# First score group of a causal attention: 112 and 224 key columns instead of 256

## The chip, the cores and the metric

The kernel runs on one core of one Trainium2 chip. The metric is the device time of one execution in microseconds (us); the time of a kernel is the median over its runs. Shapes are written as partitions x elements, and `128x448` for a matmul means 128 contraction rows and 448 moving columns.

## The reference, cut to what matters

A causal attention (2 batches, 12 heads, 448 positions, head size 64) is followed by two MLP-mixer-like blocks, the second with a two-dimensional Fourier transform and a layer normalisation. The change touches the attention alone:

```python
scores = scale * np.matmul(q, k.transpose(0, 1, 3, 2))          # 448 x 448 for each head
mask = np.triu(np.ones((seq, seq), dtype=bool), k=1)
scores = np.where(mask, -1000000000.0, scores)
scores = scores - np.max(scores, axis=-1, keepdims=True)
attn = np.exp(scores)
attn = attn / (np.sum(attn, axis=-1, keepdims=True) + 1e-09)
return np.matmul(attn, v)
```

Query block `i` of 112 positions needs only the first `112 * (i + 1)` keys; all later ones are masked.

## The kernel before, in words

The 24 heads of both batches are worked on as 12 pairs. Of a pair, one head's 64 rows of q and k lie in partitions 0 to 63 and the other's in 64 to 127, so that two matmuls, one for each head (`e` in the code), lie in two halves of TensorE's array. The 448 queries are cut into four blocks of 112.

For precision q and k are split into a high and a low part (`qh`, `ql`, `kh`, `kl`, type fp32r, a rounded fp32), and each score is the sum of three matmuls: high times high, high times low, low times high.

`scores(n, g)` makes the scores of pair `n` in three groups: `g` = 0 holds query blocks 0 and 1, `g` = 1 block 2, `g` = 2 block 3. The results of a group lie in one PSUM bank for each head. In group 0 block 1 stands in columns 0 to 255 and block 0 in columns 256 to 511. After the products, matmuls of a bf16 identity with a bf16 mask (line 234) add -1e9 above the diagonal. VectorE takes the negated maximum of each row (line 238), and ScalarE makes the exponential with that maximum as its bias and sums the row (line 247). Both read only the `112 * (i + 1)` columns that the block needs; line 214 sets the width of the matmuls on its own:

```python
for i, c0 in zip(blocks, cols):
    w = max(256, TS * (i + 1))
```

With `TS` = 112 that gives 256, 256, 336 and 448 columns for the four blocks. Line 221 is the matmul of these products.

The order of TensorE's instructions is written out by hand in a loop over `n`: scores group 0 of pair `n`, then the product with the values (`pv`, line 275, plain fp32) of pair `n` - 2, scores group 1 of pair `n`, and then transposes of the probabilities (line 260) of pair `n` - 1 around scores group 2, with parts of the first mixer block (lines 321, 333, 355) and the transposes of the outputs (line 296) put between. VectorE and ScalarE carry the softmax, copies out of PSUM (lines 265 and 267), and the conversion of float64 weights to two fp32r parts (lines 75 to 93). The feed-forward layers behind the attention (lines 134 to 136 and 497 to 499) are long rows of matmuls of 448 columns. Line 709, in a later stage, multiplies by a single column to get variances.

Of the kernel before, what the change touches and what calls it, by code (L numbers as in the profile page):

```python
# [21 lines left out]
TS = 112  # L22
# [18 lines left out]
def fused_kernel(ctx: ExitStack, tc: tile.TileContext, qk, v, w1, w2, wa, wb, wc, wd, fa, fa0, fb, out):  # L41
# [100 lines left out]
    with ExitStack() as actx:  # L142
        ps = actx.enter_context(tc.tile_pool(name="aps", bufs=2, space=bass.MemoryType.PSUM))

        def ybank():
            return ps.tile([128, 512], F32, tag="y", name="b_y")
# [56 lines left out]
        def scores(n, g):  # L203
            c = pairs[n]
            if g == 0:
                c.ssum = ap.tile([TS, NI, 2, 1], F32, tag="ssum", name="ssum", bufs=3)
                c.nmx = ap.tile([TS, NI, 2, 1], F32, tag="nmx", name="nmx")
                c.p = ap.tile([TS, 2, 1120], F32, tag="p", name="p")
            if n or g < 2:
                sp = ps.tile([128, 2, 512], F32, tag="s", name="b_s", bufs=2)  # L210
                se = [sp[:TS, e] for e in range(2)]
            else:
                se = [ybank()[:TS] for e in range(2)]
            cols = ((256, 0), (0,), (0,))[g]
            blocks = ((0, 1), (2,), (3,))[g]
            for i, c0 in zip(blocks, cols):
                w = max(256, TS * (i + 1))
                for m, (qt, kt) in enumerate(((c.qh, c.kh), (c.qh, c.kl), (c.ql, c.kh))):
                    for e in range(2):
                        he = slice(D * e, D * e + D)  # L220
                        mm(  # L221
                            se[e][:, c0 : c0 + w], lhsT=qt[he, i * TS : (i + 1) * TS], rhs=kt[he, :w],
                            start=m == 0 and i != 1, stop=False, skip_group_check=True,
                        )
            for hb in range(2):
                for e in range(2):
                    he = slice(D * e, D * e + TS // 2)
                    if g == 0:
                        dst = se[e][:, TS : TS + 288].rearrange("p (i n) -> p i n", i=2)[:, :, :TS]
                        rhs = maskb[he, hb]  # L230
                    else:
                        dst = se[e][:, blocks[0] * TS : (blocks[0] + 1) * TS]
                        rhs = maskb[he, hb, 0]
                    mm(dst, lhsT=identb[he, hb], rhs=rhs, start=False, stop=hb == 1, skip_group_check=True)
            for i, c0 in zip(blocks, cols):
                w = TS * (i + 1)
                if n or g < 2:
                    mark[2] = vec.tensor_reduce(  # L238
                        out=c.nmx[:, i], in_=sp[:TS, :, c0 : c0 + w], axis=AX.X, op=ALU.max, negate=True
                    ).ins  # L240
                else:
                    for e in range(2):
                        vec.tensor_reduce(out=c.nmx[:, i, e], in_=se[e][:, :w], axis=AX.X, op=ALU.max, negate=True)
            for i, c0 in zip(blocks, cols):
                w = TS * (i + 1)
                for e in range(2):
                    mark[3] = act.activation(  # L247
                        out=c.p[:, e, OFF[i] : OFF[i] + w], in_=se[e][:, c0 : c0 + w], func=AF.Exp,
                        bias=c.nmx[:, i, e], scale=1.0, accum_out=c.ssum[:, i, e],
                    ).ins  # L250
# [164 lines left out]
        with tc.manual_schedule(engines={mybir.EngineType.PE}):  # L415
            for n in range(np_ + 2):
                live, old = n < np_, 1 <= n <= np_
                if live:
                    scores(n, 0)
# [9 lines left out]
                if live:  # L429
                    load_v(n)  # L430
                    scores(n, 1)
# [11 lines left out]
                if live:  # L443
                    scores(n, 2)
# [388 lines left out]
```

## Time and profile before

| | |
|---|---|
| median of 3 runs | 740.5 us (740.07 to 741.49) |
| span of the profiled execution, first to last instruction | 734.8 us |
| the runs against that span | 5.3 to 6.7 us above it, 5.7 by the median |
| mean granted TensorE clock in the profile | 0.992 of full speed |
| TensorE busy in the profile | 704.3 us |
| VectorE busy in the profile | 521.9 us |

The profile is of one execution. Its span has no start and end of the program around it, which the times of the runs have; of the profiled execution itself only the span is known. Busy shares are averages over stages with different limits.

### The profile page before, as it was taken

The numbers are of one execution on the slowest core, as the hardware profiler recorded it, in microseconds if no ns is written. First come the engines' busy times: TensorE is split into PE (matmuls) and PEld (weight loads), VectorE is DVE, ScalarE is ACT, GpSimd is POOL, SyncE is SP. The second block draws the span as 40 slices with busy tenths as digits, with TensorE's granted clock in tenths as the row PEclk, the third lists the DMA queues.
The fourth block names the chain that finished last, engine by engine and source line by source line (L and its number), as shares of the span: only waits on it lengthen the run. The fifth ranks groups of instructions, "written<-read, shape, count | busy, mean of one in ns | idle before, by whom it ended". The sixth has DMA issues, their size and how long they took to land.

```text
span 734.8 us, 10275 instructions
## 1 busy us (share of the span) xinstructions
PE 704.3 (96%) x3940; PEld 629.0 (86%) x3940; DVE 521.9 (71%) x808; ACT 285.6 (39%) x600; POOL 274.6 (37%) x197
## 2 busy tenths in 40 slices
PE   6879899999999999999799999999999999999997
PEld 5657677788899999998599999999999999999996
DVE  6788887455798795678979996767745686944722
ACT  7786767332323332224353352233332222432200
POOL 3143543354233241251287334465223546321210
PEclk9999999999999999999999999999999999999999
DMA  8252401019434332300022333333321434322311
GB/s 263 55 154 68 137 26 56 29 62 269 136 123 140 119 117 98 109 22 0 1 86 87 116 121 109 129 129 116 121 79 58 144 124 135 115 86 83 111 50 51
DMA packets 20608, 74.11 MB, mean 101 GB/s; under 512 B 2364, under 2 KB 6974, under 8 KB 20192
## 3 DMA queue, kind: packets, MB, share of 16 engines
q1 hardware_dynamic: 19952, 69.48, 29.3%
q0 software_dynamic: 608, 3.99, 1.9%
q8 instruction: 31, 0.51, 0.3%
q14 instruction: 17, 0.14, 0.1%
HBM read 70.70 MB, written 2.75 MB: 100 GB/s over the span
## 4 chain that ended last, share of the span: by engine, by line
PE 76%; DVE 12%; ACT 5%; DMA 2%; POOL 2%; issue 2%; SPq 0%; ACTq 0%; DVEq 0%; POOLq 0%
PE b_s L136 6%; PE b_s L134 6%; PE b_s L135 6%; PE b_s L497 5%; PE b_s L498 5%; PE b_s L499 5%; PE b_t L499 3%; PE b_t L497 3%; PE b_t L498 3%; PE b_t L134 3%; PE b_t L136 3%; PE b_t L135 3%; PE b_s L221 2%; ACT p L247 2%; PE b_t L260 2%; PE b_y L275 2%
## 5 line engine op out<-in xcount | busy, mean ns | idle before, releaser
L93 POOL TENSOR_TENSOR wl<-m,wh 128x512 fp32r<-128x512 f32 (+1 forms) x90 | 149.0, 1657 | 261.8 <-ACT wh L92 248.6
L75 ACT ACTIVATE m<-w 128x512 f32<-128x512 f32 (+2 forms) x92 | 71.3, 775 | 158.7 <-POOL wl L93 123.1
L77 DVE TENSOR_SCALAR m<-m 128x512 f32<-128x512 f32 (+2 forms) x92 | 51.9, 565 | 91.9 <-ACT m L75 91.8
L82 DVE SCALAR_TENSOR_TENSOR m<-w,m 128x512 uint32<-128x512 uint32 (+2 forms) x92 | 101.7, 1107 | 2.4
L92 ACT CAST wh<-m 128x512 fp32r<-128x512 f32 (+1 forms) x90 | 63.3, 704 | 97.2 <-DVE m L86 46.7
L86 DVE SCALAR_TENSOR_TENSOR m<-w,m 128x512 uint32<-128x512 uint32 (+2 forms) x92 | 97.2, 1057 | 1.5
L134 PE MATMUL b_s<-acth,wh 128*128 128x448 f32 x240 | 88.2, 367 | 1.5 <-DVE resid L357 1.5
L135 PE MATMUL b_s<-acth,wl 128*128 128x448 f32 x240 | 87.9, 366 | 0.0
L136 PE MATMUL b_s<-actl,wh 128*128 128x448 f32 x240 | 87.8, 366 | 0.0
L497 PE MATMUL b_s<-gh,wh 128*128 128x448 f32 x208 | 76.2, 366 | 0.0
L498 PE MATMUL b_s<-gh,wl 128*128 128x448 f32 x208 | 75.9, 365 | 0.0
L499 PE MATMUL b_s<-gl,wh 128*128 128x448 f32 x208 | 75.7, 364 | 0.0
L247 ACT ACTIVATE p<-b_s,nmx 112x112 f32<-112x112 f32 (+3 forms) x94 | 45.2, 493 | 23.9 <-DVE nmx L238 19.9
L738 POOL TENSOR_TENSOR resid<-t,resid 128x448 f32<-128x448 f32 x24 | 33.6, 1402 | 49.5 <-DVE t L737 49.5
L78 DVE TENSOR_SCALAR m<-m 128x512 uint32<-128x512 uint32 (+2 forms) x92 | 49.6, 540 | 2.2
L134 PEld LDWEIGHTS b_s<-acth,wh 128*128 128x128 f32 x240 | 45.1, 188 | 5.7 <-issue 1.9
L136 PEld LDWEIGHTS b_s<-actl,wh 128*128 128x128 f32 x240 | 45.1, 188 | 4.0
L135 PEld LDWEIGHTS b_s<-acth,wl 128*128 128x128 f32 x240 | 45.1, 188 | 3.9
L497 PE MATMUL b_t<-gh,wh 128*128 128x448 f32 x120 | 44.0, 367 | 1.1 <-ACT gh L137 1.1
L498 PE MATMUL b_t<-gh,wl 128*128 128x448 f32 x120 | 43.8, 365 | 0.0
L499 PE MATMUL b_t<-gl,wh 128*128 128x448 f32 x120 | 43.7, 364 | 0.1
L260 PE MATMUL b_t<-ident,p 112*112 112x112 f32 x240 | 31.5, 270 | 12.0 <-DVE pt L267 6.9
(260 smaller groups left out, 1537.2 us busy)
## 6 DMA issues: line engine op xcount, KB each, us to landing
w<-in_wc SPq DMA_DIRECT2D x24, 768.0 KB, 4.3
w<-in_wd SPq DMA_DIRECT2D x36, 512.0 KB, 3.3
w<-in_wa SPq DMA_DIRECT2D x12, 768.0 KB, 4.2
w<-in_wb SPq DMA_DIRECT2D x18, 512.0 KB, 3.3
resid<-in_qk SPq DMA_DIRECT2D x24, 224.0 KB, 2.8
v<-in_v SPq DMA_DIRECT2D x12, 224.0 KB, 2.7
out<-t SPq DMA_DIRECT2D x12, 224.0 KB, 1.9
w<-in_w SPq DMA_DIRECT2D x2, 896.0 KB, 9.2
```

The source lines that it names most:

```text
L75: act.activation(out=m, in_=hi.bitcast(F32), func=AF.Abs)
L82: vec.scalar_tensor_tensor(out=mu, in0=lo, scalar=29, in1=mu, op0=ALU.logical_shift_right, op1=ALU.bitwise_or)
L86: vec.scalar_tensor_tensor(out=mu, in0=hi, scalar=0xC0000000, in1=mu, op0=ALU.bitwise_and, op1=ALU.bitwise_or)
L92: act.copy(wh, m)
L93: pool.tensor_tensor(out=wl, in0=m, in1=f(wh), op=ALU.subtract)
L134: mm(pb[:, :S], lhsT=lh, rhs=act_h[ct][b], start=ct == 0, stop=False)
L135: mm(pb[:, :S], lhsT=ll, rhs=act_h[ct][b], start=False, stop=False)
L136: tail[0] = mm(pb[:, :S], lhsT=lh, rhs=act_l[ct][b], start=False, stop=ct == NCT - 1).ins
L247: mark[3] = act.activation(out=c.p[:, e, OFF[i] : OFF[i] + w], in_=se[e][:, c0 : c0 + w], func=AF.Exp, bias=c.nmx[:, i, e], scale=1.0, acc ...
L497: mm(pb[:, :S], lhsT=lh, rhs=gh, start=j + k == 0, stop=False)
L498: mm(pb[:, :S], lhsT=ll, rhs=gh, start=False, stop=False)
L499: tail[0] = mm(pb[:, :S], lhsT=lh, rhs=gl, start=False, stop=j == last and k == nk - 1).ins
```

## The change

The width of the score matmuls is no longer raised to 256. Query block 0 is multiplied with 112 keys and block 1 with 224. Blocks 2 and 3 keep 336 and 448. The places in PSUM stay as they are.

```diff
             for i, c0 in zip(blocks, cols):
-                w = max(256, TS * (i + 1))
+                w = TS * (i + 1)
                 for m, (qt, kt) in enumerate(((c.qh, c.kh), (c.qh, c.kl), (c.ql, c.kh))):
                     for e in range(2):
                         he = slice(D * e, D * e + D)
```

## Rows read from the trace of the kernel before

**Rows 1.** The page: busy time of TensorE, and the chain by engine.
```profile
PE 704.3 (96%) x3940; PEld 629.0 (86%) x3940; DVE 521.9 (71%) x808; ACT 285.6 (39%) x600; POOL 274.6 (37%) x197
...
PE 76%; DVE 12%; ACT 5%; DMA 2%; POOL 2%; issue 2%; SPq 0%; ACTq 0%; DVEq 0%; POOLq 0%
```

**Rows 2.** Windows: stretch, length, busy time of each engine (instructions), granted clock, DMA.
```profile
0.00:134.00 134.00, 116.75 (x1027) 92.73 (x1028) 105.30 (x180) 96.50 (x284) 49.95 (x49) 0.97 0.34 104
134.00:735.00 601.00, 587.55 (x2915) 536.30 (x2913) 416.55 (x628) 189.12 (x316) 224.70 (x148) 1.00 0.31 100
```

**Rows 3.** Waits of TensorE up to 134 us: in total, times, longest.
```profile
PE b_t L260 <- DVE pt L267: 6.6, 5, 2.2
PE b_t L260 <- ACT pt L265: 5.1, 6, 1.0
```

**Rows 4.** The chain in order of time, 0 to 140 us: start, length, what.
```profile
4.56 1.96 PE b_s L221 x12
...
17.80 1.55 PE b_s L221 x11
...
27.14 0.88 PE b_s L221 x12
...
35.70 0.88 PE b_s L221 x12
...
45.44 1.00 DVE nmx L238
...
60.55 0.89 PE b_s L221 x12
...
96.18 0.89 PE b_s L221 x12
...
117.02 0.90 PE b_s L221 x12
...
134.26 0.21 PE b_s L135
```

**Rows 5.** Windows over four of the twelve first score groups.
```profile
17.73:19.15 1.42, 1.42 (x13) 1.42 (x14) 0.94 (x2) 0.97 (x3) 0.42 (x1) 0.50 0.06 17
27.07:27.86 0.79, 0.79 (x13) 0.79 (x14) 0.79 (x2) 0.06 (x1) 0.70 (x1) 1.00 0.12 14
...
46.31:47.10 0.79, 0.79 (x13) 0.79 (x14) 0.79 (x3) 0.63 (x3) 0.13 (x1) 1.00 0.00 0
...
81.28:82.69 1.41, 1.41 (x13) 1.41 (x14) 1.41 (x3) 1.41 (x5) 1.19 (x2) 0.50 0.05 12
```

**Rows 6.** Timeline of TensorE over a full-clock group: start, length, instruction.
```profile
27.28 0.28 PE L221 MATMUL b_s<-kl,qh 64*112 64x256 f32 x2
...
27.75 0.28 PE L221 MATMUL b_s<-kh,ql 64*112 64x256 f32 x2
27.86 0.35 PE L234 MATMUL b_s<-maskb,identb 56*112 56x224 bf16 x4
```

**Rows 7.** Timeline of TensorE over a group at clock 0.50.
```profile
18.09 0.41 PE L221 MATMUL b_s<-kl,qh 64*112 64x256 f32 x2
...
18.94 0.41 PE L221 MATMUL b_s<-kh,ql 64*112 64x256 f32 x2
```

**Rows 8.** The chain, 60 to 66 us: mask matmuls, four of 224 and four of 112 columns.
```profile
61.44 0.19 PE b_s L234 x4
...
64.32 0.10 PE b_s L234 x4
```

**Rows 9.** Weight loads of line 709: timeline, and durations (min/median/max ns).
```profile
427.06 0.77 PEld L709 LDWEIGHTS b_t<-mean_w,rstd 128*112 128x112 f32 x7
...
L709 PEld LDWEIGHTS b_t<-mean_w,rstd x8: 174/178/178, 426.9 to 427.6; 128*112 128x112 f32 x8
```

**Rows 10.** TensorE by line and form: busy us, mean ns of one, idle before.
```profile
L275 PE MATMUL b_y<-pt,v 112*64 112x224 f32 x48 | 6.6, 352 | 0.0
...
L275 PE MATMUL b_y<-pt,v 112*64 112x112 f32 x48 | 4.3, 259 | 0.0
```

## Prediction

> **What bounds the kernel now.** I read the page first: TensorE is busy for 96% of the span, and 76% of the chain of work that ended last runs on it [rows 1]. I then split the span where attention ends and the feed-forward layers begin, because the changed matmuls all lie in front of that point. Up to 134 us TensorE works for 116.75 us, VectorE for 105.30 and ScalarE for 96.50; after it TensorE works for 587.55 of 601 us [rows 2]. So whatever the attention stage gains or loses at its end is handed on nearly whole, but inside the stage three engines take turns at being last, and TensorE is kept waiting by the copies of the transposed probabilities (6.6 and 5.1 us) [rows 3]. A saving on TensorE counts there only where the chain runs through it.
>
> The changed work is the first score group of each of the 12 head pairs: 12 matmuls (two query blocks, three products, two heads), all 256 keys wide. The chain passes through seven of the twelve groups: those at 4.56, 17.80, 27.14, 35.70, 60.55, 96.18 and 117.02 us [rows 4]. In the other five (the one that starts at 46.31 us is an example, [rows 5]) it runs through VectorE and ScalarE; a row of that kind is the key reduction at 45.44 us [rows 4].
>
> **What one matmul costs now.** The two heads sit in the two halves of the array and start together, so a "x2" row is one step. At full clock the starts run from 27.28 to 27.86: 0.58 us for five steps, 116 ns a step [rows 6]. Streaming the same number of columns at 2.4 GHz is 107 ns; about 10 ns is overhead. The group that starts at 17.73 has a granted clock of 0.50 [rows 5] and a step of 213 ns, from 18.09 to 18.94 in four steps [rows 7]. The group at 81.28, off the chain, has 0.50 too [rows 5], and the one at 4.56 is as slow, 1.96 us in the chain against 0.88 or 0.89 for a full-clock group [rows 4]. So I count three slow groups, two of them on the chain, and nine at full clock, five on the chain.
>
> **The change, step by step.** No instruction is added, removed or moved. Per pair, six matmuls go from 256 to 112 columns and six from 256 to 224. VectorE's maximum and ScalarE's exponential already read 112 and 224 columns, the mask matmuls write inside them, and no transfer or queue is touched. The columns that are no longer written are read by nobody. So the only cost in dispute is the step of a matmul of this operand type (rounded fp32) at 224 and at 112 columns, and the trace has none narrower than 256. I bound it from both sides.
>
> - Lower bound: the bf16 mask matmuls in the same two-head arrangement. Two steps at 112 columns take 0.10 us and two at 224 take 0.19 [rows 8], 50 and 95 ns a step. That would be 66 and 21 ns less than now.
> - A floor under the narrow one: each matmul brings its own 112 weight columns of four bytes. In the variance stage a run of fp32 matmuls of a single moving column has to load 112 weight columns for each, so the loads alone set its pace: seven of them, 178 ns long each, overlap within 0.77 us [rows 9], and (770 - 178) / 6 is a new one every 98 ns. A step of 112 columns therefore cannot be expected under some 98 ns. At 224 columns, 93 ns of streaming plus 10 of overhead is 103, just above it.
> - Upper bound: plain fp32 at these very widths, in the product of probabilities and values. The code makes 24 products per width and the trace shows 48 records, so each product is two passes; the mean record goes from 259 to 352 ns between 112 and 224 columns, 93 ns for every 112 [rows 10]. Per product that is 187 ns at 112 columns and 373 at 224.
>
> I take 98 and 103 ns: the matmul of this type already ran at one column per cycle at 256, as it does not at plain fp32, and the weight load is the only thing in these rows that does not shrink with the columns. Per full-clock group: 3 x ((116 - 98) + (116 - 103)) = 93 ns. In a slow group I let weight load and stream take twice as long (about 187 to 195 ns a step against 213), which saves 3 x (20 + 20) = 0.12 us. All twelve groups: 9 x 0.093 + 3 x 0.12 = 1.2 us of TensorE time. On the chain: 5 x 0.093 + 2 x 0.12 = 0.7 us. The five off the chain only lengthen idle time that TensorE already has. Some of it may still help, since an earlier maximum lets VectorE go on earlier: at most the whole 1.2.
>
> The Trainium skill's page "TensorE: Matmul & The Clock Gate", section "Back-to-back issue gap", gives a warm gap of N/2.4 + 2.5 ns for a matmul by itself; an estimate from it is 49 ns at 112 columns and 96 at 224, and a saving of 3.1 us over the 36 steps of each kind, against my 1.2. The loads of the one-column matmuls, 98 ns apart [rows 9], do not go by it.
>
> The profiled span of 734.8 becomes 734.1. The runs lie 5.7 us above that span by the median, and nothing outside the span changes: 740.5 - 0.7 = **739.8 us**. That is -0.1%, and under the 0.2% (1.5 us) that a measurement of this kernel can tell from no change.
>
> **Rivals.**
> - *Slower: the narrow form falls back to the pace of plain fp32.* What speaks for it is that the four-byte operands are the same as in those two-pass products, and that all matmuls of the fast type in this trace have at least 256 columns, so nothing here shows that the fast pace holds below. Against it stands that the pace keeps to the columns as far as the trace goes: 0.21 us at 448 [rows 4] and 0.116 at 256 [rows 6] are both some 0.46 ns a column. With 187 and 373 ns: 3 x ((187 - 116) + (373 - 116)) = 0.98 us per full-clock group; a slow one up to twice that, 1.7 as I take it, since the longer group runs out of the slow stretch. On the chain 5 x 0.98 + 2 x 1.7 = 8.3 us; for all twelve, if TensorE's waits [rows 3] hide nothing, 9 x 0.98 + 3 x 1.7 = 13.9. So 749 to 754 us. It decides (1.5 us more) once a 224-column step costs between some 165 ns, with all groups counted, and 190, with those on the chain alone.
> - *Half of that: one record, but two cycles a column.* 98 and 187 ns: 3 x (71 - 18) = 0.16 us more per full-clock group and 3 x (160 - 20) = 0.42 in a slow one. On the chain 5 x 0.16 + 2 x 0.42 = 1.6, in all 2.7: 742.1 to 743.2 us, just slower. For it: a record of fp32 in [rows 10] has this pace. Against it: the fast type at 256 has twice the pace.
> - *Faster: the weight load hides.* By the mask rows, 3 x (66 + 21) = 0.26 us per full-clock group and 3 x (113 + 23) = 0.41 in a slow one, 2.1 us on the chain and 3.6 in all: 736.9 to 738.4 us. For it: today the loads of both heads lie under one step [rows 6]. Against it: [rows 9], and the mask's weights have two bytes instead of four.
> - *The clock tips.* A slow group costs 1.42 us instead of 0.79 [rows 5]. TensorE came to the slow stretch near 17.7 us out of its waits on the copies. With a little less to stream, such a stretch can appear once more or once less: 0.6 us per such group, and with its neighbours some 1.5 us either way. The three runs already spread over 1.4 us.
>
> **How the numbers follow.** Forecast (weight load sets the step) 0.50, plain fp32 pace 0.30, two cycles a column 0.10, hidden weight load 0.05, a tip of the clock 0.05. The likeliest case alone spans 738.5 to 741.2: 739.8 with the 1.2 us of full effect on one side and the spread of the runs on the other. For 8 in 10 the range must take in the hidden load at its lesser effect, the two-cycle case, and the lower part of the fp32 case: 738.2 to 750.5. Faster by over 0.2%: most of the hidden load, half of the clock and an eighth of the forecast, 0.12. Slower: the fp32 case, most of the two-cycle case and half of the clock's, 0.39. Within: 0.49.
>
> **What would show it.** Right: the two kinds of score matmul keep one record each, with steps near 98 and 103 ns, a full-clock group shrinks from 0.79 to about 0.70 us, the feed-forward layers begin some 0.7 us earlier and their stretch is as long as before. Wrong: a 112-column step near 187 and a 224-column one near 373 ns, or twice as many records for line 221 (fp32); steps of 50 and 95 (hidden load); another list of stretches at 0.50 (clock). The forecast also fails if the time gained is eaten by a wait on VectorE behind the same group, which would leave 740.5.

## The result and the profile after

The changed kernel takes 745.55 us (median of 6 runs, 743.29 to 747.88) against 740.65 (6 runs, 739.29 to 741.49): a ratio of 1.0071, with a 95% interval from 1.0052 to 1.0091. Twelve later runs of it gave 744.57 against 740.04, 1.0055 [1.0035, 1.0075]. It is slower by some 0.6%. The forecast was 739.8 us, a small gain that no measurement could tell from no change. The ratios here and below are those of the record; they are not exactly the quotients of the two medians.

The steps in dispute came out as forecast. The timeline of TensorE in the changed kernel, over a full-clock first group (start, length, instruction):

```profile
31.26 0.31 PE L221 MATMUL b_s<-kh,qh 64*112 64x112 f32 x2
31.41 0.26 PE L221 MATMUL b_s<-kl,qh 64*112 64x112 f32 x2
31.50 0.26 PE L221 MATMUL b_s<-kh,ql 64*112 64x112 f32 x2
31.60 0.31 PE L221 MATMUL b_s<-kh,qh 64*112 64x224 f32 x2
31.75 0.27 PE L221 MATMUL b_s<-kl,qh 64*112 64x224 f32 x2
31.86 0.26 PE L221 MATMUL b_s<-kh,ql 64*112 64x224 f32 x2
31.96 0.36 PE L234 MATMUL b_s<-maskb,identb 56*112 56x224 bf16 x4
```

Two steps at 112 columns take 0.19 us (31.41 to 31.60), 95 ns each; two at 224 take 0.21 (31.75 to 31.96), 105 each. Forecast were 98 and 103, where [rows 6] have 116. The first step of each width takes longer, 0.15 us (31.26 to 31.41, 31.60 to 31.75); before, only the first step of the group did, 0.21 us (from 27.07 in [rows 5] to 27.28 in [rows 6]). The forecast had neither; in the sum over a group the two nearly cancel. There is one record for each matmul, as before. The windows over this group and over one at clock 0.50 are the rows that answer to [rows 5]:

```profile
20.29:21.55 1.26, 1.26 (x13) 1.26 (x14) 0.73 (x2) 1.07 (x3) 0.16 (x1) 0.50 0.00 0
...
31.26:31.96 0.70, 0.70 (x14) 0.70 (x15) 0.70 (x2) 0.00 (x0) 0.70 (x1) 1.00 0.12 10
```

0.70 us instead of 0.79, and 1.26 instead of 1.42. Yet the profiled execution is longer. Its span is 11.3 us above that of the profile before, more than twice the 4.9 us between the medians, because the one is the longest of six runs and the other was shorter than usual (see below). The page of the changed kernel:

```profile
span 746.1 us, 10275 instructions
...
PE 713.3 (96%) x3940; PEld 634.6 (85%) x3940; DVE 520.8 (70%) x808; ACT 286.0 (38%) x600; POOL 273.9 (37%) x197
```

The number of instructions is the same, and TensorE is busy for 9 us *more* than in [rows 1]. Windows of the changed kernel show why: four stretches at half the clock (0.50, the level of 1.2 GHz) within attention, and the two parts that answer to [rows 2].

```profile
15.30:25.50 10.20, 9.39 (x52) 6.22 (x54) 4.78 (x10) 7.86 (x27) 1.13 (x1) 0.50 0.32 122
...
49.40:56.20 6.80, 6.54 (x36) 4.56 (x38) 6.17 (x12) 3.39 (x13) 2.41 (x2) 0.50 0.23 70
...
87.00:93.80 6.80, 6.80 (x40) 3.95 (x40) 5.62 (x13) 4.97 (x16) 3.75 (x4) 0.50 0.23 70
...
124.50:127.90 3.40, 3.40 (x20) 1.60 (x18) 3.20 (x8) 1.98 (x11) 1.28 (x1) 0.50 0.01 2
...
0.00:142.70 142.70, 124.01 (x1028) 96.15 (x1029) 104.02 (x181) 96.86 (x284) 49.34 (x49) 0.90 0.33 98
142.70:746.10 603.40, 589.28 (x2914) 538.44 (x2912) 416.77 (x628) 189.16 (x316) 224.56 (x148) 0.99 0.31 100
```

Attention ends 8.7 us later than in [rows 2] (142.70 against 134.00), at a mean clock of 0.90 instead of 0.97; what follows is 2.4 us longer, at 0.99 instead of 1.00.

And something else has changed that the edit does not name: the order of VectorE's instructions. Its timeline in the kernel before, around pair 1 (L238 is a maximum, L292 and L293 the row sums of pair 0, L195 the low part of pair 2's queries, L267 a copy of transposed probabilities):

```profile
10.88 0.92 DVE L238 TENSOR_REDUCE nmx<-b_s 112x2 f32<-112x224 f32 x2 [0.33 <-PE b_s L234]
11.94 0.17 DVE L292 TENSOR_SCALAR ssum<-ssum 112x8 f32<-112x8 f32 x1
12.14 0.20 DVE L293 RECIPROCAL ssum<-ssum 112x8 f32<-112x8 f32 x1
12.26 0.81 DVE L238 TENSOR_REDUCE nmx<-b_s 112x2 f32<-112x672 f32 x1
12.99 1.06 DVE L195 SCALAR_TENSOR_TENSOR ql<-resid,qh 128x448 fp32r<-128x448 f32 x1
13.97 0.61 DVE L267 COPY pt<-b_t 112x448 f32<-112x448 f32 x1
```

The same in the changed kernel:

```profile
11.82 0.17 DVE L292 TENSOR_SCALAR ssum<-ssum 112x8 f32<-112x8 f32 x1 [1.68 <-ACT p L247]
12.03 0.20 DVE L293 RECIPROCAL ssum<-ssum 112x8 f32<-112x8 f32 x1
12.75 1.18 DVE L195 SCALAR_TENSOR_TENSOR ql<-resid,qh 128x448 fp32r<-128x448 f32 x1 [0.52 <-ACT qh L191]
13.85 1.67 DVE L238 TENSOR_REDUCE nmx<-b_s 112x2 f32<-112x224 f32 x3
15.44 0.61 DVE L267 COPY pt<-b_t 112x448 f32<-112x448 f32 x1
```

The maxima of pair 1 did not overtake the row sums. VectorE now waits 1.68 us for ScalarE's exponentials of pair 0 and 0.52 for its conversion of pair 2's queries, while the scores of pair 1, whose reading began at 10.88 before, lie ready from about 10.61, when their last matmuls end. The maxima start at 13.85, the exponentials of pair 1 behind them and the copy at 15.44 instead of 13.97, and TensorE's longest wait for that copy goes from the 2.2 us of [rows 3] to 3.8. TensorE's two rows on either side, and its waits in the changed kernel:

```profile
10.26 0.35 PE L234 MATMUL b_s<-maskb,identb 56*112 56x224 bf16 x4
...
16.11 1.00 PE L260 MATMUL b_t<-ident,p 112*112 112x112 f32 x4 [3.77 <-DVE pt L267]
```

```profile
PE b_t L260 <- DVE pt L267: 8.5, 5, 3.8
```

In pairs 2 to 4 the row sums have moved ahead of the maxima too. In pair 3, the kernel before and then the changed one:

```profile
28.93 0.43 DVE L304 CAST xh<-x 112x512 fp32r<-112x512 f32 x1
29.27 0.92 DVE L238 TENSOR_REDUCE nmx<-b_s 112x2 f32<-112x224 f32 x2
30.10 1.70 DVE L82 SCALAR_TENSOR_TENSOR m<-w,m 112x1024 uint32<-112x1024 uint32 x1
31.72 0.16 DVE L292 TENSOR_SCALAR ssum<-ssum 112x8 f32<-112x8 f32 x1
```

```profile
33.12 0.43 DVE L304 CAST xh<-x 112x512 fp32r<-112x512 f32 x1
33.46 0.16 DVE L292 TENSOR_SCALAR ssum<-ssum 112x8 f32<-112x8 f32 x1
33.66 0.20 DVE L293 RECIPROCAL ssum<-ssum 112x8 f32<-112x8 f32 x1
33.78 0.87 DVE L238 TENSOR_REDUCE nmx<-b_s 112x2 f32<-112x224 f32 x2
```

Counted from the start of the cast, the maxima start 0.34 us later before, and 0.66 now. Two later pairs have changed as well: in pair 5 a reciprocal comes a little earlier, and in pair 8 the row sums (89.48 to 89.87 us) stand ahead of the first maxima, where before they came after them. On ScalarE, GpSimd and SyncE the order of the two traces is the same.

The order on VectorE is not written out in the kernel, as TensorE's is, apart from a few places that an `issue_after` fixes. The rest is made when the program is built; since the edit changes nothing but widths and the order came out another way, it presumably goes by expected durations. So two theories stood against each other. *Order*: the loss comes from VectorE's new order and the waits it brings. *Columns*: the narrow groups themselves let TensorE's clock be lowered more often.

### The profile page after: what moved, and what is told of

The parts are those of the page before. It is cut to its first block, busy times and chain, and to the rows that moved or that the text cites. A ratio compares the mean times of both kernels' runs of the same rounds, so it can differ in the third digit from the quotient of the medians.

```text
span 746.1 us, 10275 instructions
## 1 busy us (share of the span) xinstructions
PE 713.3 (96%) x3940; PEld 634.6 (85%) x3940; DVE 520.8 (70%) x808; ACT 286.0 (38%) x600; POOL 273.9 (37%) x197
## 4 chain that ended last, share of the span: by engine, by line
PE 78%; DVE 12%; ACT 4%; DMA 2%; issue 2%; POOL 2%; ACTq 0%; POOLq 0%; DVEq 0%; SPq 0%
PE b_s L134 6%; PE b_s L136 6%; PE b_s L135 6%; PE b_s L497 5%; PE b_s L498 5%; PE b_s L499 5%; PE b_y L275 3%; PE b_t L499 3%; PE b_t L497 3%; PE b_t L498 3%; PE b_s L221 3%; PE b_t L260 3%; PE b_t L134 2%; PE b_t L136 2%; PE b_t L135 2%; PE b_y L321 2%
```

## The experiments

Most runs have a mean granted clock on record, and the traces show two levels, 1.00 and 0.50 (2.4 and 1.2 GHz). So 2 x (1 - clock) x span is the time that an execution spent at the low level. Over all 286 executions of this study that have one, a straight line with one slope and a level of its own for each kernel gives **0.30 us of run time for each us at the low clock** (standard error 0.01; what is left scatters by 1.0 us). With it a difference in time splits into the clock's part and the rest, "at equal clock"; the split is this fit's, and it takes one slope for all kernels. The table has the medians and ratios as measured on the same chip, then the mean time at the low clock with its standard error, and the difference to the kernel before (120 executions) at equal clock with its 95% interval. The unchanged kernel itself came out at a ratio of 1.0017 when it was measured again, so a ratio of that size shows nothing. On the four chips used, the kernel before has 18.5, 20.8, 19.3 and 21.7 us at the low clock, each with a standard error of 0.7 to 1.0, so part of a difference of 2 or 3 us can be the chip's.

| kernel | us | ratio to before | us at low clock | at equal clock |
|---|---|---|---|---|
| before, all executions | 739.1 to 740.7 | | 20.0 ± 0.4 | 0 |
| again: before, unchanged | 739.91 | 1.0017 [1.0000, 1.0034] | 20.7 ± 1.0 | +0.2 ± 0.6 |
| changed, first 6 runs | 745.55 | 1.0071 [1.0052, 1.0091] | 30.5 ± 2.2 | +2.6 ± 0.9 |
| changed_again | 744.57 | 1.0055 [1.0035, 1.0075] | 26.4 ± 1.7 | +2.7 ± 0.6 |
| narrow_old_order | 740.42 | 1.0009 [0.9987, 1.0031] | 25.1 ± 1.8 | -1.2 ± 0.6 |
| narrow_old_again | 740.30 | 1.0008 [0.9988, 1.0028] | 25.0 ± 2.1 | -1.0 ± 0.6 |
| wide_new_order | 743.24 | 1.0043 [1.0022, 1.0063] | 25.1 ± 2.0 | +1.8 ± 0.6 |
| wide_both | 741.26 | 1.0021 [1.0003, 1.0038] | 21.1 ± 0.9 | +1.5 ± 0.6 |
| narrow_from_third | 742.99 | 1.0044 [1.0021, 1.0068] | 27.7 ± 1.2 | +0.9 ± 0.6 |
| narrow_first_two | 742.44 | 1.0043 [1.0025, 1.0061] | 23.1 ± 1.6 | +1.3 ± 0.7 |
| narrow_q_fixed | 744.04 | 1.0068 [1.0043, 1.0093] | 29.2 ± 1.7 | +1.4 ± 0.9 |
| narrow_sums_fixed | 743.49 | 1.0049 [1.0029, 1.0068] | 25.7 ± 1.5 | +1.3 ± 0.6 |
| narrow_filled | 740.38 | 0.9991 [0.9972, 1.0010] | 21.9 ± 1.2 | -0.7 ± 0.6 |
| wide_filled | 739.85 | 0.9996 [0.9981, 1.0011] | 18.5 ± 1.0 | +0.3 ± 0.6 |
| narrow_more | 740.95 | 1.0018 [1.0001, 1.0036] | 22.2 ± 1.4 | +1.0 ± 0.6 |
| wide_more | 742.06 | 1.0032 [1.0011, 1.0052] | 19.0 ± 1.4 | +2.4 ± 0.6 |

**again and changed_again: the two kernels once more.** No edit.

> The kernel before, unchanged, to see the span and the granted clock of several executions. Order theory and column theory alike: 740.5 us (739 to 741.5) and a mean clock near 0.99.

> The changed kernel, unchanged, for more executions on the same chip as the next three. 744.5 to 746.5 us, mean clock 0.98.

The kernel before has 20 us at the low clock in the mean, not the 12 that the same formula gives for the profile that the prediction read (three stretches of 3.4 us and the end of its span). The changed one has 26 to 31.

**narrow_old_order: the change, with VectorE's order held.** The low part of pair 2's queries is made behind the second group of pair 1, and `issue_after`, which fixes the order of a queue and adds no wait, puts the row sums behind the next pair's first maxima. `pairs[n + 1].first` is the last maximum of that pair's first group.

```diff
                     scores(n, 1)
+                    if n == 1:
+                        low_q(2, pairs[2].q32)      # taken out of prep(2), behind mark[2]
...
+            with ExitStack() as order:
+                if n < 4 or n == 7:
+                    order.enter_context(tc.issue_after(pairs[n + 1].first))
-            vec.tensor_scalar(out=c.ssum, in0=c.ssum, scalar1=1.0e-9, scalar2=None, op0=ALU.add)
-            vec.reciprocal(out=c.ssum, in_=c.ssum)
+                vec.tensor_scalar(out=c.ssum, in0=c.ssum, scalar1=1.0e-9, scalar2=None, op0=ALU.add)
+                vec.reciprocal(out=c.ssum, in_=c.ssum)
```

> All twelve first groups narrow (112 and 224 columns), with VectorE's instructions held in the order of the kernel before, except two instructions of 0.2 us. Order theory (the loss comes from the low part of pair 2's queries, which VectorE now makes ahead of pair 1's maxima, and from the slow clock that follows this wait): 739.5 to 740.5 us. Column theory (fewer streamed columns let the clock of TensorE be lowered more often in all pairs): 744 to 746 us, mean clock 0.98.

740.42 us, no difference to before, as the order theory forecast. Over the whole program VectorE's order is that of the kernel before but for two instructions, a reciprocal near 49 us and a cast near 84, and the other queues are unchanged. VectorE's timeline around pair 1 is the old one again (the lines of the code have moved: L245 is a maximum, L304 and L305 the sums, L202 the queries, L276 the copy):

```profile
10.66 0.92 DVE L245 TENSOR_REDUCE nmx<-b_s 112x2 f32<-112x224 f32 x2
12.00 0.17 DVE L304 TENSOR_SCALAR ssum<-ssum 112x8 f32<-112x8 f32 x1 [0.41 <-ACT p L256]
12.20 0.20 DVE L305 RECIPROCAL ssum<-ssum 112x8 f32<-112x8 f32 x1
12.32 0.81 DVE L245 TENSOR_REDUCE nmx<-b_s 112x2 f32<-112x672 f32 x1
13.04 1.06 DVE L202 SCALAR_TENSOR_TENSOR ql<-resid,qh 128x448 fp32r<-128x448 f32 x1
14.03 0.61 DVE L276 COPY pt<-b_t 112x448 f32<-112x448 f32 x1
```

So with the same widths the order makes 4.2 us (744.57 against 740.42, on two chips whose kernel before differs by 0.2). At equal clock the narrow groups *save* 1.2 us, and the repeat gives 1.0, each within 0.6; the forecast was 0.7, at most 1.2. But 25 us at the low clock instead of 20 cost 1.5 us, and the saving is gone.

**narrow_old_again: the same once more.**

> The narrow kernel with VectorE's old order once more, for the size of what is left without the order: 739.5 to 741 us if the order is the cause, and more time at the low clock than the kernel before (some 25 us against 19).

740.30 us and 25.0 us at the low clock: both findings hold.

**wide_new_order: 256 columns with the new order in pair 1.** The row sums of pair 0 come ahead of pair 1's maxima with it. One more `issue_after`, not shown, keeps ScalarE's order as it was. Unlike in the changed kernel, the low part of pair 3's queries comes behind the last maxima of pair 1 (at 21.05 us, the maxima at 18.84).

```diff
+                if n == 1:
+                    prep(2)
                 if live:
                     scores(n, 0)
...
+                        if n == 1 and g < 2:
+                            order.enter_context(tc.issue_after(pairs[2].low))   # pair 2's low queries
                         mark[2] = vec.tensor_reduce(
```

> 256 columns everywhere, as before, but VectorE makes the low part of pair 2's queries ahead of pair 1's maxima, as in the changed kernel. Order theory: 744 to 746 us, with the first transposes of pair 0 waiting some 3.7 us instead of 2.2. Column theory: 740 to 742 us, the added wait of 1.6 us at most.

743.24 us, slower by 0.43% with not one column taken away: above the column theory's 740 to 742, and short of the order theory's 744 to 746. Its waits of TensorE have the long one, as forecast (some 3.7):

```profile
PE b_t L263 <- DVE pt L273: 8.1, 5, 3.8
```

**wide_both: 256 columns with the row sums moved ahead as well.** The sums get a function of their own, called ahead of the first group of pairs 2 to 4, and that group's maxima are put behind it. The low part of pair 3's queries came to stand a little later than in the changed kernel, a conversion on ScalarE moved by a few places, and the sums of later pairs stayed in the old place, those behind pair 8's first maxima among them.

```diff
+                if n in (1, 2):
+                    prep(n + 1)
+                if n in SUMS:              # (2, 3, 4)
+                    sums(n - 1)
                 if live:
                     scores(n, 0)
```

> 256 columns everywhere, with VectorE's order of the changed kernel in pairs 1 to 4: the low part of pair 2's queries ahead of pair 1's maxima, and the row sums of the pair before ahead of the first maxima of pairs 2, 3 and 4. Order theory: 744 to 746.5 us, above the 743.2 of the run that moved the first of the two alone. Column theory (the loss is in the narrow steps themselves or in the clock that they cause): 740 to 743.5 us.

741.26 us. This missed the order theory's 744 to 746.5 and lies in the column theory's range, and its 0.21% is hardly more than the 0.17% of the unchanged kernel's repeat. At equal clock it agrees with the first part alone (+1.5 and +1.8), and both are clear of 0; the time between the two is the clock. So with wide groups the moved sums cost nothing of their own that could be seen.

**narrow_from_third and narrow_first_two: the change in ten pairs, and in two.** One line replaces the first one shown, in each of the two runs.

```diff
-                w = max(256, TS * (i + 1))
+                w = TS * (i + 1) if n >= 2 else max(256, TS * (i + 1))    # narrow_from_third
+                w = TS * (i + 1) if n < 2 else max(256, TS * (i + 1))     # narrow_first_two
```

> Pairs 0 and 1 keep 256 columns, the ten others are narrow; VectorE's order in pair 1 is that of the kernel before. Order theory: 739.5 to 740.5 us. Column theory: 743.5 to 745.5 us.

> Only pairs 0 and 1 are narrow; VectorE's order in pair 1 is that of the changed kernel, all later pairs are as before. Order theory: 742 to 744 us, although ten of the twelve pairs are unchanged. Column theory: 740 to 741 us.

Both are slower by 0.4%. With the first two pairs alone narrow, only pair 1's order changes on VectorE (maxima behind the sums and the queries), and that is enough for +1.3 us at equal clock: the order follows the widths, though the lines of VectorE's work are the same. With the ten later pairs narrow, pair 1 keeps its old order and the sums move from pair 2 on. This missed the expectation of the order theory as I had put it, which counted pair 1 alone: here the sums do cost, +0.9 at equal clock where ten twelfths of the saving would give -0.9. The measured 742.99 lies between the ranges of the two theories. Pair 8's sums have moved in this run, too.

**narrow_q_fixed and narrow_sums_fixed: half of the order each.** These take the first or the second half of the edit of narrow_old_order.

> Narrow first groups; the low part of pair 2's queries is put back behind pair 1's maxima, but the row sums of the pair before stay ahead of the first maxima of pairs 1 to 4, as in the changed kernel. If each part of the order costs for itself: 741.5 to 743.5 us, between the narrow kernel in the old order (740.2) and the changed one (744.5). If the query part alone is the cause: 739.5 to 741 us.

> Narrow first groups; the row sums are put back behind the first maxima, but the low part of pair 2's queries stays ahead of pair 1's maxima. If each part of the order costs for itself: 741.5 to 743.5 us. If the sums alone are the cause: 739.5 to 741 us.

744.04 us, above its range of 741.5 to 743.5, and 743.49, at the end of it. With either part left in the new order the kernel is slow: against the narrow kernel in the old order (-1.1), the sums cost 2.5 us at equal clock and the queries 2.4, and both together 3.8. That the whole is less than the sum of the parts fits pair 1, where the two delay the same maxima, though the 1.1 us between them are no more than their error. These start at 12.14 us with the sums alone ahead (narrow_q_fixed, first row) and at 13.93 with the queries alone (second row), against 13.85 with both:

```profile
12.14 1.64 DVE L245 TENSOR_REDUCE nmx<-b_s 112x2 f32<-112x224 f32 x3
```

```profile
13.93 0.91 DVE L238 TENSOR_REDUCE nmx<-b_s 112x2 f32<-112x224 f32 x2
```

The sums of narrow_q_fixed stand in the new place in pair 8 as well, as in the changed kernel and in narrow_from_third. In wide_both, where the moved sums cost nothing, they do not. No run moves pair 8's sums alone, so how much of the 2.5 us arises there is open.

**narrow_filled and wide_filled: TensorE kept at work in three waits.** Four matmuls, whose result nobody reads, go ahead of the third unit of transposes in the iterations of pairs 1 to 3. The order on all other engines stays as it is (narrow_filled against narrow_old_order, wide_filled against the kernel before).

```diff
+        def fill(n):
+            c = pairs[n]
+            pb = ybank()
+            for k in range(4):
+                mm(pb[:, :S], lhsT=c.kh[:, :128], rhs=c.qh, start=k == 0, stop=k == 3)
...
+                if n in (1, 2, 3):
+                    fill(n)
                 if old:
                     transposes(n - 1, 2)
```

> Narrow first groups with the old order of VectorE, and four matmuls of 448 columns whose result nobody reads, put in each of the iterations of pairs 1, 2 and 3 where TensorE waits for the copies of the transposed probabilities. Clock theory (an idle TensorE in these waits brings the slow clock, and narrow groups make it likelier): time at the low clock falls by 4 to 8 us from 25, 737.5 to 739.5 us. Rival (the clock is lowered by something else, or the waits are not where it is decided): 740 to 741.5 us, the same clock.

> The kernel before with the same unread matmuls in the same places. Clock theory: 737 to 739.5 us, time at the low clock 3 to 6 us less than the 19 to 21 of the kernel before. Rival: 740 to 741 us.

The profiles of both have no low stretch near 16 us. They run at full clock up to some 42 us, in the iteration after the last filled one, and there the clock falls. Windows of wide_filled:

```profile
8.40:42.60 34.20, 29.74 (x292) 22.31 (x290) 29.02 (x50) 28.90 (x95) 9.35 (x7) 1.00 0.53 159
42.60:49.40 6.80, 5.56 (x32) 4.34 (x34) 5.98 (x12) 3.30 (x10) 2.54 (x3) 0.50 0.25 61
```

That the filling did this is not shown. A single profile of each kernel says where its low stretches lie in one execution only, and the unfilled narrow kernel does the same without help: in narrow_old_again the clock is full from 14 to 22 us (first row), and narrow_old_order has a low stretch at 42.5 us besides one at 15.2 (second row, its later one).

```profile
14.00:22.00 8.00, 7.36 (x43) 5.19 (x44) 4.67 (x10) 5.00 (x16) 1.13 (x1) 1.00 0.56 212
```

```profile
42.50:49.20 6.70, 5.90 (x40) 4.77 (x40) 6.10 (x9) 4.42 (x13) 2.47 (x2) 0.50 0.32 119
```

What all executions show is smaller. The narrow kernel has 3 us less at the low clock in the mean (21.9 against 25.0), the wide one 1.5; each difference is within twice its error, and both are less than the 4 to 8 and 3 to 6 that were forecast. The times, 740.38 and 739.85 us, miss the clock theory's ranges and cannot be told from the kernel before. narrow_filled, the fastest that these findings pointed to, does not beat it (0.9991, interval on both sides of 1).

**narrow_more and wide_more: columns given back, or added.** Query block 2 is made for 448 keys; the last 112 are not read.

```diff
-                w = max(256, TS * (i + 1))
+                w = (256, 256, S, S)[i]       # wide_more
+                w = (TS, 2 * TS, S, S)[i]     # narrow_more, in the old order
```

> Narrow first groups in VectorE's old order (three other small instructions move in later pairs), with query block 2 made for 448 keys instead of 336, of which the last 112 are not read: some of the columns taken out of the first group are streamed again in the second, at 47 ns a step. If the number of streamed columns sets how often the clock is lowered: time at the low clock falls from 25 us to 19 to 22. If not: 24 to 26 us. Either way about 1 us more of plain TensorE work, 740 to 741.5 us in all.

> The kernel before, with query block 2 made for 448 keys instead of 336: more streamed columns than in the kernel before, and a few small instructions of VectorE and ScalarE change places. If the number of streamed columns sets how often the clock is lowered: time at the low clock 14 to 18 us instead of 19 to 20. If not: 19 to 21 us. 739.5 to 741.5 us.

narrow_more has 22.2 us at the low clock, less than the 25.0 without those columns by 2.9 with a standard error near 1.9. wide_more has 19.0, near the kernel before (20.0) and above the 14 to 18 that were forecast if columns decide. The direction fits the column theory in the first, and neither difference is clear of its error. At equal clock narrow_more is 2.1 us above the narrow kernel, near the 36 steps x 47 ns = 1.7 us that it adds. wide_more, 742.06 us, is slower than its forecast of 739.5 to 741.5, +2.4 at equal clock. That is 0.7 above the added columns, and it is no clean test: in pair 1 the low part of pair 2's queries has again moved ahead of the maxima of the second group, and a copy on ScalarE has changed places.

## Why the prediction was wrong

- **The matmul's step** was right: 95 and 105 ns for 98 and 103, no fall back to the pace of plain fp32, one record each. That the sum over a group came out at 0.09 us is in part luck, since the longer first steps were not in it. The Trainium skill's page "TensorE: Matmul & The Clock Gate" has both sides of this: an estimate from the formula in "Back-to-back issue gap" for a matmul by itself is 49 ns at 112 columns, and the section says of it that at small widths it counts too little, because it leaves out the weight load; this trace has 95. An estimate from its section "LDWEIGHTS (loading the stationary operand)" is 93 ns for a load of 112 columns; the pace of 95 at full clock agrees. The record of a single load lasts longer, 178 ns in [rows 9]; successive loads overlap.
- **The saving** was right: 0.7 to 1.2 us forecast, 1.0 and 1.2 at equal clock, each within 0.6, once the order is held.
- **"No instruction is added, removed or moved" was wrong, and it is the step that failed.** The edit moved VectorE's row sums and the low part of pair 2's queries ahead of maxima that were ready. Holding the order takes the loss away (narrow_old_order), and making it without the edit brings a loss (wide_new_order). It costs 3.8 us at equal clock with narrow groups: +2.7 with the new order, -1.1 with the old one. With wide groups the parts of it that were made cost 1.5 to 1.8. The prediction did name a wait on VectorE behind the same group as a way to fail, but as one that only eats the gain and leaves 740.5.
- **The clock** was a rival with a chance of 0.05 and 1.5 us to either side. Its price was about right for the narrow groups in the old order (5 us more at the low clock, 1.5 us). The changed kernel has 26.4 to 30.5 us, in the mean over its 18 runs 27.8, which is 7.8 more than before and costs 2.3. The chance was far too low, and it was not to either side.
- Together: -1.1 (steps) + 3.8 (order) + 2.3 (clock) = +5.0 us; 4.9 was the difference of the medians first measured. The split is the fit's, so the sum must come out; what stands without a fit is 744.57 against 740.42.
- **The range**, 738.2 to 750.5 us, holds the 745.55 by luck: its upper part was there for the pace of plain fp32, which did not occur.
- **The base** was read from a lucky execution. I took the 5.7 us between span and median as something outside the span. In every execution whose span is on record the run is 1.8 us longer than it. Of the other 3.9 us, the 12 us at the low clock instead of 20 account for some 2.4 by the fit; the remaining 1.5 is of the size of the scatter that the fit leaves (1.0 us). It did no harm to the sum, but it hid how much of the kernel's time the clock decides.
- **Not settled**: why the narrow groups in the old order spend 25 us at the low clock and not 20. That they do is shown by 24 executions against 120 (5.1 us, standard error 1.4). They have fewer columns, but that the columns are the reason is not shown: filling or streaming more brings about half to all of it back, and each such difference is hardly twice its error. I did not try to shift the groups against the clock's changes in time. Also open is why the order costs 3.8 us with narrow groups and 1.5 to 1.8 with wide ones, where it was not made in full (pair 3's queries, pair 8's sums).

## What to carry to other kernels

Where one engine's order is written out and another's is made when the program is built, an edit of a size on the first can reorder the second: compare the order of all queues before you count an edit as "nothing moved", and hold the order when you measure a size. What to look for is an instruction with a late input that now stands ahead of one that the chain waits for: here VectorE stood still for 1.68 and 0.52 us behind two such instructions. And before reading a profile as the kernel's usual state, compare its mean clock and span with those of several runs.

## What the hardware showed that I had not expected

- The scatter goes mostly with the clock: executions of the kernel before lie between 735.6 and 745.0 us, and with the time at the low clock taken out 1.0 us is left. A us at the low clock goes with 0.30 us of run time, less than the 0.5 that half the clock would cost a TensorE always at its limit. In the first low stretch of the changed kernel TensorE is busy for 9.39 of 10.20 us, so it is not always at its limit; that this makes up the difference was not tested.
- The rounded-fp32 matmul kept its pace of one column per cycle down to 224 columns, 105 ns a step with some 12 over the streaming. At 112 columns the step is 95 ns. That the weight load sets it is inferred from the 98 ns between loads in [rows 9]. In a slow group the step is 190 ns for both widths (20.52, 20.71 and 20.90; 21.36 and 21.55 as starts in the changed kernel), as forecast, so at 112 columns it doubles with half the clock.
- Where the low stretches lie varies from one execution to the next: two profiles of the same narrow kernel in the old order have their first one at 15.2 and at 45.5 us. In the changed kernel's profile the first one begins at 15.3 us, in the 3.77 us in which TensorE waits. The Trainium skill's page "TensorE: Matmul & The Clock Gate" describes in "A second HAM failure mode: psum-queue depth-cycling" a kernel in which short idle times between groups of matmuls make the clock go back and forth. No run here shows that such a wait brings the fall.
